# Attention loads over all 128 partitions, the block means through the tensor engine for every pair, an earlier expert pick and a linear part inside the test

## The chip, the cores and the metric

The kernel runs on one NeuronCore of a Trainium2 chip. The metric is device time in microseconds (us) of one execution. TensorE (PE), VectorE (DVE), ScalarE (ACT), GpSimd (POOL) and SyncE (SP) each have an instruction queue of their own. SP issues every load and store here but one; the bytes are moved by 16 DMA engines.

## The reference, cut to what matters

```python
def _attn_ref(q, k, v):                       # q, k, v: (4, 8, 768, 64)
    k_sum = k.reshape(B, H, nb, 32, D).max(axis=3)
    v_sum = v.reshape(B, H, nb, 32, D).mean(axis=3)
    scores = concat(window scores |i-j| < 16, q @ k_sum.T + log(32))
    return softmax(scores) @ concat(v, v_sum)
def _moe_ref(x, phi, w1, w2):                 # x: (3072, 512), 8 experts, 4 slots each
    logits = x @ phi
    slot_input = softmax(logits, axis=0).T @ x
    slot_out[e] = relu(slot_input[e] @ w1[e]) @ w2[e]
    return softmax(logits, axis=1) @ slot_out
def _moe2_ref(x, expert_emb, tau, w1, w2):    # top-1 expert for each token
    expert_idx = argmax(xn @ en.T / tau)
    out = gate * (relu(x @ w1[e]) @ w2[e])
```

The output of the attention is the x of the first mixture, whose output is the x of the second. All tensors are float32.

## The kernel before

**Attention.** The 4 x 8 heads are taken as 16 pairs of heads n. Each pair has 3 steps u = 3n, 3n+1, 3n+2, so there are 48 steps. A step scores 4 query blocks of 64 rows for both heads (`s_pe`, L351), takes maximum and exponential (`s_max`, `s_exp`), transposes the probabilities (`p_pe`, L386) and multiplies them with the values (`v_pe`, L403). The parts are staggered over the steps: `p_pe` of step u-2, `v_pe` of step u-3. Every three steps PE also transposes the result and adds the logits of the first mixture (L436, L454); after every batch of four pairs it adds `pn` and `pa` (L497, L525).

A pair loads q (`qT`, 128 rows), k (`kT`, 128 rows, written as six pieces of 512 bytes in each row, between which the block maxima of k stand) and a windowed copy of v, `vw`. Its tile has up to 120 rows: the window rows of the even and the odd query blocks, and in rows 16 to 39 (even) and 80 to 103 (odd) the 24 block means of v. The load of `vw` is three or four transfers: 120, 80 and 16 rows for pairs 0 to 7 (`VS_PE`), 16, 80, 80 and 16 rows for pairs 8 to 15 (L266).

The block means come about in two ways. For pairs 0 to 7, PE forms them from `vw` itself (`vs_pe`, L278, four products), ACT takes them out of PSUM (`vs_out`, L289), SP writes them to DRAM (`vsp`, L296), waits for that write, and reads them back into `vw` in two transfers that repeat them six times (`vsum_in`, L318). For pairs 8 to 15, v is loaded once more for two pairs at a time in 96 rows (`load_vs`, L256), POOL adds its halves (L304), SP writes the means (`vsc`, L311) and reads them back. The source calls in step u are in the order: `vs_pe`, `vs_out`, `vs_dma`, the loads of k and q, the load of v two pairs ahead, the read-back, one load of a weight tile.

**Weights.** From step 9 on one tile of 1 MB of the first mixture's weights is loaded per pair (`load_w`, L177); 32 tiles in all, the last ones as buffers come free. 16 products `ph` (L800) and 16 pieces `pO` (L866) use them up; r counts two groups of four experts, fc the eight pieces of a group.

**Second mixture.** Because one expert serves all tokens where the inputs allow it, the kernel picks the expert of token 0 before the last pieces are added: behind piece fc = `G_STEP` = 5 of the second group it copies the sum so far, multiplies it out for token 0 (`first_expert`: `px`, `pl`, then DVE makes the index `ei`), and SP loads that expert's weights (`w1e`, `w2e`, L828, L835). The last two pieces go into a second bank; `psoT` (L920) adds both halves in the transpose. Then come a Gram matrix (`pk`, L950), 8 tokens' logits (`pl`, L955), the product of the slot outputs with `w1e` (`pg`, L1029, `pgs`, L1042), which makes G, and the other logits. `norms` and `codes` on DVE end the stage.

**Test.** 24 pieces `pht` (L1113) of G times the tokens are checked for sign, 14 on ACT (L1132) and 10 on DVE (`T_DVE`, L1121), over a ring of four double banks. Where all tokens agree in sign, a hidden unit is linear; the linear part is `prr` (L1158), `rs`, `prs` (L1207) and `RR` (L1222). The units that are not linear are gathered (`prk`, `OH`, `pix`, `pgm`, an indirect load `wr`), and the output loop adds three products for them to the linear product `linear` (L1230), scales and stores (L1248). A loop behind that runs a whole expert for each further expert that tokens chose.

```python
G_STEP = 5                                            # L44
return psb.tile([P, 1024], F32, tag=f"d{n2[0] % 4}", name=name)   # L1107
```

Of the kernel before, what the change touches and what calls it, by code (L numbers as in the profile page):

```python
# [31 lines left out]
NSLOT = 32  # L32
NBIG = 15
NBIG2 = 4

VS_PE = (0, 1, 2, 3)
# [7 lines left out]
G_STEP = 5  # L44

T_DVE, T_GATES, T_OTHERS = (5, 7, 9, 11, 13, 15, 17, 19, 21, 23), (6, 8, 10, 13), 15
NE = 8
# [89 lines left out]
def tile_kernel(ctx, tc, qT, kTd, vwd, vbd, phi, w1, w2, emb, tau, u1, u2, consts, consts2, out):  # L137
# [68 lines left out]
    with ExitStack() as es:  # L206
# [18 lines left out]
        vos = []  # L225
# [14 lines left out]
        def load_qk(n):  # L240
            if n == 0:
                for h in range(2):
                    nc.sync.dma_start(
                        out=k_blocks(0)[:, 3 * h : 3 * h + 3, 0:128],
                        in_=kTd[0, :, h * 384 : h * 384 + 384].rearrange("p (c x) -> p c x", x=P),
                    )
# [52 lines left out]

        def vsum_add(m):  # L300
            vs = st_["vs", m]
            h = BLK // 2
            while h:
                nc.gpsimd.tensor_add(vs[:, :h, :], vs[:, :h, :], vs[:, h : 2 * h, :])  # L304
                h //= 2

        def vsum_out(m):
            vo = vos[m % 2]
            nc.gpsimd.tensor_scalar_mul(vo[:, 0:D], st_.pop(("vs", m))[:, 0, :], 1.0 / BLK)
            sc = dram.tile([NB, 2, 130], F32, name=f"vsc{m}")  # L310
            nc.sync.dma_start(out=sc.rearrange("n i (j d) -> (n i j) d", j=2), in_=vo)  # L311
            for i in range(2):
                st_["sc", 2 * m + i] = sc[:, i, :]
# [334 lines left out]
        for u in range(NU + 32):  # L648
# [59 lines left out]
            for n in range(NPAIR):  # L708
                if n // 2 in VS_PE:
                    up, uo, ui = VS_FIRST[n] if n < 2 else (3 * n - 2 - (n % 4 == 3), 3 * n - 1, 3 * n)  # L710
                    if u == up:
                        vs_pe(n)
                        vs_out(n)
                    if u == uo:
                        vs_dma(n)
                    if u == ui and n == 0:
                        load_qk(2)
                        vsum_in(0)
                    elif u == ui:
                        late.append(n)  # L720
# [8 lines left out]
            if (m := at(u, 0, 6, 2 * B - 1)) is not None and m + 1 not in VS_PE:  # L729
                load_vs(m + 1)  # L730
            if (m := at(u, 3, 6, 2 * B - 1)) is not None and m + 1 not in VS_PE:
                vsum_add(m + 1)
            if (m := at(u, 5, 6, 2 * B - 1)) is not None and m + 1 not in VS_PE:
                vsum_out(m + 1)
            if (n := at(u, 6, 3, NPAIR - 2)) is not None and (n + 2) // 2 not in VS_PE:
                vsum_in(n + 2)
# [78 lines left out]
    OO = [O, hx[:, 5, :]]  # L815
# [42 lines left out]
    for r in range(2):  # L858
        for fc in range(8):
# [3 lines left out]
            for c in range(2):  # L863
# [54 lines left out]
    for c in range(4):  # L918
        for i in range(2):
            nc.tensor.matmul(  # L920
                pt[:, c * P : (c + 1) * P], OO[i][:, c * P : (c + 1) * P], sel, start=i == 0, stop=i == 1
            )
# [163 lines left out]
    pgs = [g_half(f, bank) for f in range(2)]  # L1086
    pg = [g_sum(f, pgs[f], bank) for f in range(2)]
    for f in range(2):
        g_parts(f, pg[f])
    for t in range(8, NTT):  # L1090
        tok(t)
    ph0 = bank(1, "ph0")[:, 0 : 2 * NU].rearrange("p (k x) -> p k x", x=2)
    for k in range(NU):
        nc.tensor.matmul(ph0[:, k, :], G[:, k * P : (k + 1) * P], cTt(0, 2), start=True, stop=True)
    nc.vector.tensor_scalar(out=pos, in0=ph0[:, :, 0], scalar1=0.0, scalar2=None, op0=ALU.is_ge)
    nc.vector.tensor_scalar(out=ngs, in0=pos, scalar1=-2.0, scalar2=1.0, op0=ALU.mult, op1=ALU.add)
    norms()
    codes()
    psa_es.close()

    with ExitStack() as es:
# [3 lines left out]
        def dbank(name):  # L1105
            n2[0] += 1
            return psb.tile([P, 1024], F32, tag=f"d{n2[0] % 4}", name=name)  # L1107

        for i in range(3 * NU):
# [25 lines left out]
            if i == 4:  # L1135
# [19 lines left out]
        prr, rs = dbank("prr")[:, 0:512], hx[:, 1, :]  # L1155
        for k in range(NU):
            g = k % 4
            nc.tensor.matmul(  # L1158
                prr[32 * g : 32 * g + 32, :], GPT[:, k, :], w2e[k // 4][:, k % 4, :], start=k < 4, stop=k >= 4
            )  # L1160
        nc.scalar.copy(rs, prr)

# [10 lines left out]
    for k in range(NU):  # L1173
# [6 lines left out]
        )  # L1180
    nc.vector.scalar_tensor_tensor(
# [153 lines left out]
```

## Time and profile before

| | us |
|---|---|
| median of 3 runs | 325.37 |
| lowest, highest | 320.84, 325.95 |
| the profiled execution | 324.63 |
| its span, from the first to the last instruction | 322.5 |
| PE, DVE, ACT, POOL busy | 270.8, 168.9, 156.7, 40.0 |

The profile is of one execution. A row of the chain or of the timeline gives the start, the duration, the engine, the tile written, the line, and how many instructions were merged (x8). A matmul of float32 counts twice. A row of the windows view gives a stretch, then the busy time of the engines asked for, then the clock that TensorE was granted (1.00 is 2.4 GHz, 0.50 is 1.2 GHz), the busy share of the DMA engines and GB/s. "SPq" is the time that SP's queue needs to issue a transfer.

### The profile page before, as it was taken

To read this page: it belongs to the slowest core of one execution; us is meant where nothing else is said; L and a number is where in the kernel's file an instruction comes from. 1 tells how busy PE (TensorE), PEld (TensorE's weight loads), DVE (VectorE), ACT (ScalarE), POOL (GpSimd) and SP (SyncE) were. 2 spreads that over 40 slices of the span, in tenths; PEclk is the share of its full clock that TensorE was granted. 3 is DMA by queue.
4 is the path that set the end of the run, shared out by engine and by line. 5 is a ranking of instruction groups with operands and counts; after the bars stand their busy time and mean duration, and the time that the engine had idled before them with its cause. 6 is when DMAs were issued, how large, how long until landed. Compare 5 with 4: busy or idle time off the path is not lost.

```text
span 322.5 us, 6780 instructions
## 1 busy us (share of the span) xinstructions
PE 270.8 (84%) x2428; PEld 183.9 (57%) x2428; DVE 168.9 (52%) x756; ACT 156.7 (49%) x390; POOL 40.0 (12%) x63
## 2 busy tenths in 40 slices
PE   6779999939994994994988999999987778778890
PEld 2556877718784873684875643354544544555560
DVE  3546677733985475484584542141215489345440
ACT  2554887816685563484684621132312797133330
POOL 2000010102512413413400001000000030100000
PEclk9589999987999897897899999999978798769997
DMA  7999798899997996998988999999394000105563
GB/s 196 211 258 239 215 277 267 206 275 244 220 267 187 287 310 182 286 293 225 310 217 232 387 387 384 387 386 381 116 363 158 2 0 0 33 31 194 201 254 112
DMA packets 49342, 74.00 MB, mean 229 GB/s; under 512 B 4048, under 2 KB 22416, under 8 KB 48920
## 3 DMA queue, kind: packets, MB, share of 16 engines
q1 hardware_dynamic: 49224, 73.26, 76.4%
q8 instruction: 21, 0.34, 0.5%
q0 software_dynamic: 80, 0.26, 0.3%
q14 instruction: 17, 0.14, 0.2%
HBM read 67.02 MB, written 6.49 MB: 228 GB/s over the span
## 4 chain that ended last, share of the span: by engine, by line
PE 52%; DMA 28%; DVE 6%; ACT 5%; SPq 4%; issue 3%; DVEq 0%; ACTq 0%
DMA vsc<-vo 12%; DMA vw<-in_vw_dram 7%; PE s L351 7%; PE po L403 5%; PE pO L866 5%; PE ph L800 4%; DMA vsp<-vo 4%; PE pt L386 3%; PE pa L525 3%; PE py L1230 3%; DMA qn<-in_qT_dram 2%; PE tx L436 2%; DMA vw<-vsc 2%; DVE hlo L1121 2%; PE pv L278 2%
## 5 line engine op out<-in xcount | busy, mean ns | idle before, releaser
L351 PE MATMUL s<-fix,fix 128*128 128x120 f32 x384 | 60.5, 305 | 3.5 <-DVE nb L363 3.0
L351 PEld LDWEIGHTS s<-fix,fix 128*128 128x128 f32 x384 | 51.4, 208 | 16.4 <-issue 5.2
L403 PE MATMUL po<-vw,pts 120*64 120x65 f32 x768 | 35.7, 232 | 18.0 <-DMA vw<-vsc 15.7
L391 ACT COPY pts<-pt 120x512 f32<-120x512 f32 x48 | 28.1, 585 | 37.2 <-PE pt L386 36.6
L403 PEld LDWEIGHTS po<-vw,pts 120*64 120x64 f32 x768 | 28.5, 141 | 30.4 <-issue 14.4
L378 ACT ACTIVATE fix<-fix,nb 128x120 f32<-128x120 f32 x128 | 40.1, 387 | 2.6 <-DVE nb L363 2.4
L363 DVE CUSTOM_DVE_ANT_0 fix<-s,con 128x120 f32<-128x120 f32 x128 | 28.4, 277 | 19.2 <-PE s L351 16.2
L304 POOL TENSOR_TENSOR vs<-vs 96x1024 f32<-96x1024 f32 (+4 forms) x20 | 20.4, 1021 | 47.6 <-DMA vs<-in_vb_dram 46.4
L1113 PE MATMUL pht<-cT,gs 128*128 128x512 f32 x48 | 17.1, 496 | 7.0 <-DVE hx L973 3.1
L418 DVE TENSOR_SCALAR den<-po 128x4 f32<-128x4 f32 x48 | 7.5, 157 | 26.5 <-PE po L403 26.4
L420 DVE TENSOR_TENSOR X<-po,den 128x256 f32<-128x256 f32 x48 | 20.4, 424 | 1.7
L378 ACT ACTIVATE sm<-sm,nb 128x120 f32<-128x120 f32 x64 | 20.0, 387 | 0.6 <-DVE nb L363 0.5
L1132 ACT ACTIVATE hhi<-pht,ngs 128x1024 fp32r<-128x1024 f32 x14 | 15.6, 1116 | 8.0 <-PE pht L1113 7.8
L386 PE MATMUL pt<-con,fix 128*120 128x128 f32 x128 | 19.3, 273 | 0.0
L363 DVE CUSTOM_DVE_ANT_0 sm<-s,con 128x120 f32<-128x120 f32 x64 | 14.3, 277 | 7.2 <-PE pt L386 3.6
L1113 PEld LDWEIGHTS pht<-cT,gs 128*128 128x128 f32 x48 | 10.3, 236 | 13.3 <-DVE acc L1121 4.8
L436 PE MATMUL tx<-con,X 128*128 128x128 f32 x96 | 17.1, 290 | 0.0
L337 DVE TENSOR_REDUCE fix<-fix 128x12 f32<-128x384 f32 x32 | 16.2, 547 | 0.9 <-DMA fix<-in_kT_dram 0.8
L866 PE MATMUL pO<-w,hx 128*32 128x256 f32 x256 | 16.1, 383 | 0.0
L363 DVE DVE_READ_ACCUMULATOR2_ANT nb<- 128x1 f32 x192 | 15.8, 82 | 0.1
L446 ACT COPY xT<-tx 128x512 f32<-128x512 f32 (+1 forms) x32 | 14.8, 462 | 2.1 <-PE tx L436 2.1
L1121 DVE CUSTOM_DVE_ANT_0 hlo<-pht,ngs 128x1024 fp32r<-128x1024 f32 x10 | 12.2, 1215 | 6.1 <-PE pht L1113 5.3
(232 smaller groups left out, 397.4 us busy)
## 6 DMA issues: line engine op xcount, KB each, us to landing
w<-in_moe_w_dram SPq DMA_DIRECT2D x30, 1024.0 KB
out_dram<-Y SPq DMA_DIRECT2D x24, 256.0 KB
vw<-in_vw_dram SPq DMA_DIRECT2D x24, 243.8 KB
fix<-in_kT_dram SPq DMA_DIRECT2D x15, 384.0 KB
qn<-in_qT_dram SPq DMA_DIRECT2D x8, 384.0 KB
vs<-in_vb_dram SPq DMA_DIRECT2D x4, 768.0 KB
vw<-in_vw_dram SPq DMA_DIRECT2D x8, 365.6 KB
fix<-in_qT_dram SPq DMA_DIRECT2D x7, 384.0 KB
```

Of the source, the lines that this page charges most:

```text
L304: nc.gpsimd.tensor_add(vs[:, :h, :], vs[:, :h, :], vs[:, h : 2 * h, :])
L351: nc.tensor.matmul(sp[:, i, :], qbds[n % NQB][:, t, :], kTs[n % NKT][:, o : o + KW], start=True, stop=True)
L363: nc.vector.tensor_tensor_reduce(out=sm[:, i, :], in0=sp[:, i, :], in1=con[:, m0 : m0 + KW], scale=-0.125, scalar=3.0e38, op0=ALU.add, op1 ...
L378: nc.scalar.activation(sm[:, i, :], sm[:, i, :], AF.Exp, bias=nb_[:, i : i + 1], scale=-1.0)
L386: nc.tensor.transpose(pv[:, i, :], pr[:, i, :], ident)
L391: nc.scalar.copy(pts, st_.pop(("pt", u)))
L403: nc.tensor.matmul(po[64 * i : 64 * i + 64, c, j, :], pts[:, 2 * c + i, j * 64 : j * 64 + 64], vw[:, i, (t // 2) * 130 + 65 * j : (t // 2) ...
L420: nc.vector.tensor_tensor(out=X[:, 2 * g : 2 * g + 2, 2 * hp * D : (2 * hp + 2) * D].rearrange("p c (j d) -> p c j d", j=2), in0=po[:, :, ...
L436: nc.tensor.transpose(pt[:, c * P : c * P + P], st_["X", b][:, c0 + c, hp * P : hp * P + P], ident)
L866: nc.tensor.matmul(po[c][32 * g : 32 * g + 32, 0:256], hTs[r][:, fc, 32 * g : 32 * g + 32], w[:, g, cs], start=(r, fc) in ((0, 0), (1, G_S ...
L1113: nc.tensor.matmul(ph[:, c * 512 : c * 512 + 512], G[:, k * P : (k + 1) * P], cTt(1024 * j + 512 * c, 512), start=True, stop=True,)
L1121: nc.vector.tensor_tensor_reduce(out=junk[1], in0=ph, in1=ngs[:, k : k + 1].to_broadcast([P, 1024]), scale=1.0, scalar=0.0, op0=ALU.mult, ...
```

## The change

1. Loads. `kT` is laid out in DRAM as it lies in the tile, gaps included (912 floats a row, one piece). `vw` is one transfer of 128 rows x 1568 floats, with zeros where the means go; the four or three transfers are gone.
2. Block means. `VS_PE`, `load_vs`, `vsum_add` and `vsum_out` are gone: all 16 pairs take the way through PE, ACT and DRAM.
3. Pick. `G_STEP` is 3: the sum behind piece fc = 3 (of 0 to 7) is copied, `px` follows behind the products of piece 4, `pl` and the index behind those of piece 5. The remaining pieces are added on DVE to the copy, so `psoT` has one product per column block and not two.
4. Order. `pg` comes straight behind `psoT`, ahead of the Gram matrix and of all logits. The logits' banks are in a pool of their own that stays open through the test, `norms` and `codes` come behind the first test, and the test's ring has three double banks.
5. Linear part. `prr` and `rs` come behind test 17, `prs` and `RR` behind test 18; four `linear` products come ahead of `pix`. `pgm` is written twice side by side (256 columns).

```diff
-VS_PE = (0, 1, 2, 3)
-G_STEP = 5
+G_STEP = 3
+T_LIN = 17
...
-            for par, r0, r1 in (*even, (1, 0, 80), (1, 104, KW)):
-                nc.sync.dma_start(
-                    out=vw[r0:r1, par],
-                    in_=vwd[n, par, r0:r1].rearrange("p c j d -> p (c j d)"),
-                )
+            st_["vw", n] = t[:KW, :VROW].rearrange("p (a x) -> p a x", a=2)
+            nc.sync.dma_start(out=t[:, :VPAD], in_=vwd[n])
...
-            nc.sync.dma_start(out=k_blocks(n)[:, :, 0:128], in_=kTd[n].rearrange("p (c x) -> p c x", x=P))
+            nc.sync.dma_start(out=kTs[n % NKT][:, 40 : 40 + 912], in_=kTd[n])
...
                 if (r, fc) == (1, 7):
-                    (nc.scalar.copy, nc.vector.tensor_copy)[c](OO[1][:, cs], po[c][:, 0:256])
-            if (r, fc) == (1, G_STEP):
+                    nc.vector.tensor_tensor(out=O[:, cs], in0=po[c][:, 0:256], in1=O[:, cs], op=ALU.add)
+            if (r, fc) == (1, G_STEP + 1):
                 first_expert()
+            if (r, fc) == (1, G_STEP + 2):
+                first_expert_code()
...
+    pgs = [g_half(f, bank) for f in range(2)]
     gram()
-    for t in range(8):
-        tok(t)
...
-            return psb.tile([P, 1024], F32, tag=f"d{n2[0] % 4}", name=name)
+            return psb.tile([P, 1024], F32, tag=f"d{n2[0] % 3}", name=name)
...
+            if i == 0:
+                norms()
+                codes()
...
+            if i == T_LIN + 1:
+                prs = dbank("prs")[:, 0:512]
+                nc.tensor.matmul(prs, sel, rs, start=True, stop=True)
+                nc.scalar.copy(RR, prs)
+                nc.vector.tensor_tensor(out=RR[64:P], in0=prs[64:P], in1=RR[64:P].bitcast(F32), op=ALU.subtract)
```

SP's queue in the middle of the attention before, for about two pairs; `fix` and `qn` are the tiles of k and q, `w` a weight tile, `vs` the second copy of v, `vsc` the means in DRAM:

```order
L177 DMA w_1103<-in_moe_w_dram 128x4x512
L266 DMA vw_1157<-in_vw_dram 16x780
L266 DMA vw_1157<-in_vw_dram 80x780 x2
L266 DMA vw_1157<-in_vw_dram 16x780
L251 DMA fix_102<-in_kT_dram 128x6x128
L252 DMA fix_103<-in_qT_dram 128x768
L311 DMA vsc_1205<-vo_116 96x65
L256 DMA vs_1247<-in_vb_dram 96x2048
L318 DMA vw_995<-vsc_1205 24x6x130 x2
L177 DMA w_1251<-in_moe_w_dram 128x4x512
```

The same place now:

```order
L181 DMA w_1222<-in_moe_w_dram 128x4x512
L255 DMA vw_1278<-in_vw_dram 128x1568
L282 DMA vsp_1319<-vo_1276 8x390
L248 DMA fix_103<-in_kT_dram 128x912
L249 DMA qn_105<-in_qT_dram 128x768
L289 DMA vw_1134<-vsp_1319 24x6x130 x2
L181 DMA w_1360<-in_moe_w_dram 128x4x512
```

A pair now has 7 transfers on SP's queue; the means go out ahead of k and q and are read back behind them, for every pair.

PE from the pick's products to the product with the picked expert's weights before; `pc` is a transpose, `pcb` the picked code:

```order
L844 MATMUL px_2863<-c0r,O_2686 128x1
L847 MATMUL pl_2864<-enT,x_2687 1x8 x4
L196 MATMUL pc_1_2900<-con,st_2755 128x128 x3
L866 MATMUL pO_2905<-w_2627,hx 32x256 x4
L866 MATMUL pO_2906<-w_2627,hx 32x256 x4
L866 MATMUL pO_2905<-w_2633,hx 32x256 x4
L866 MATMUL pO_2906<-w_2633,hx 32x256 x4
L920 MATMUL psoT<-con,hx 128x128 x8
L950 MATMUL pk<-hx 128x40 x4
L955 MATMUL pl_2962<-KL,cT_2682 128x40 x8
L1018 MATMUL pcb<-r_2688,con 128x1
L1029 MATMUL pg_3000<-w1e_2878,hx 32x512 x2
```

The same now:

```order
L806 MATMUL px_2843<-c0r,O_2677 128x1
L200 MATMUL pc_0_2849<-con,st_2746 128x128 x3
L831 MATMUL pO_2833<-w_2605,hx 32x256 x4
L831 MATMUL pO_2834<-w_2605,hx 32x256 x4
L812 MATMUL pl_2862<-enT,x_2678 1x8 x4
L200 MATMUL pc_1_2893<-con,st_2746 128x128 x3
L831 MATMUL pO_2833<-w_2618,hx 32x256 x4
L831 MATMUL pO_2834<-w_2618,hx 32x256 x4
L831 MATMUL pO_2833<-w_2624,hx 32x256 x4
L831 MATMUL pO_2834<-w_2624,hx 32x256 x4
L886 MATMUL psoT<-con,hx 128x128 x4
L993 MATMUL pg_2968<-w1e_2871,hx 32x512 x2
```

The pick's two groups of products have a piece `pO` between them, and still two pieces follow `pl`; `psoT` has half its products, and `pg` stands where the Gram matrix stood, which with all logits now follows it.

PE at the end of the test before, the last two test pieces and what follows them:

```order
L1113 MATMUL pht_3181<-cT_2683,gs 128x512
L1113 MATMUL pht_3185<-cT_2683,gs 128x512 x2
L1158 MATMUL prr<-w2e_2880,scr 32x512 x4
L1158 MATMUL prr<-w2e_2881,scr 32x512 x4
L1172 LDWEIGHTS ltb
L1172 MATMUL prk<-flag,ltb 128x9
```

Now, test piece 17 and what follows it:

```order
L1074 MATMUL pht_3148<-cT_2674,gs 128x512 x2
L1123 MATMUL prr<-w2e_2873,scr 32x512 x4
L1123 MATMUL prr<-w2e_2874,scr 32x512 x4
L1074 MATMUL pht_3162<-cT_2673,gs 128x512 x2
L1133 MATMUL prs<-hx,con 128x512
L1074 MATMUL pht_3170<-cT_2673,gs 128x512
```

The linear part's products went from behind the last test piece (and `prs` from behind the gather) to between the pieces 17 and 19. On DVE the subtraction that makes `RR` stands ahead of test 19 in the same way.

## Rows read from the trace of the kernel before

**Rows 1.** Windows view, three stretches: stretch, length, busy of five engines, PEclk, DMA share, GB/s.
```profile
33.00:54.00 21.00, 21.00 (x254) 17.12 (x254) 15.26 (x89) 17.38 (x48) 0.82 (x1) 1.00 0.88 244
72.00:171.00 99.00, 83.34 (x896) 66.67 (x892) 62.96 (x349) 60.30 (x171) 28.86 (x34) 0.89 0.95 250
171.00:222.00 51.00, 50.88 (x538) 25.36 (x541) 19.85 (x78) 15.56 (x37) 2.04 (x4) 1.00 1.04 371
```
**Rows 2.** Windows view of PE, first 16 us: stretch, length, PE busy, PEclk, DMA share, GB/s.
```profile
9.25:11.00 1.75, 1.09 (x5) 0.50 1.15 242
11.00:12.00 1.00, 1.00 (x9) 0.50 1.07 372
12.00:15.00 3.00, 3.00 (x15) 0.50 0.94 210
```
**Rows 3.** Waits of PE on loads: us in total, times, longest.
```profile
PE po L403 <- DMA vw<-vsc: 15.7, 7, 4.6
PE pv L278 <- DMA vw<-in_vw_dram: 5.7, 3, 5.4
```
**Rows 4.** The chain in the first 36 us: start, us, what.
```profile
6.24 9.65 DMA vw<-in_vw_dram
...
25.92 6.17 DMA vw<-in_vw_dram
```
**Rows 5.** The chain through the attention, PE's score steps and one batch's end.
```profile
35.56 1.08 PE s L351 x8
...
43.97 1.08 PE s L351 x8
...
80.28 0.48 PE pn L497 x4
...
82.72 1.85 PE pa L525 x12
...
176.50 1.08 PE s L351 x8
```
**Rows 6.** Timeline of SP's queue: the means of pair 5 go out, and are read back.
```profile
53.36 0.61 SPq L296 DMA_DIRECT2D vsp<-vo  x1
...
59.93 1.91 SPq L318 DMA_DIRECT2D vw<-vsp  x2
```
**Rows 7.** The chain from the pick to the first test.
```profile
227.91 0.26 PE pO L866 x4
...
229.91 0.48 PE pc L196 x3
...
232.25 2.00 PE psoT L920 x16
...
238.45 4.04 PE pg L1029 x16
...
250.88 1.20 PE pht L1113 x2
```
**Rows 8.** Timeline of SP's queue: the loads of the picked expert's first weights.
```profile
231.89 2.19 SPq L828 DMA_DIRECT2D w1e<-in_moe_w_dram  x4
```
**Rows 9.** The test: the page's group of DVE, and of the chain its end.
```profile
L1121 DVE CUSTOM_DVE_ANT_0 hlo<-pht,ngs 128x1024 fp32r<-128x1024 f32 x10 | 12.2, 1215 | 6.1 <-PE pht L1113 5.3
...
272.74 1.92 PE prr L1158 x16
274.69 0.59 ACT hx L1161
```
**Rows 10.** The chain from the gather to the first product of the output loop.
```profile
280.18 1.81 PE prs L1207 x2
...
283.81 0.70 DVE gs L1222
284.56 2.08 PE py L1230 x4
286.64 0.43 PE py L1237
```

More of the change, by code (lines that the diff above doesn't have):

```diff
@@ L298, in vs_dma @@
             )
[L300 to L313, printed above, removed]
         def vsum_in(n):
@@ L708, in tile_kernel @@
             for n in range(NPAIR):
[L709 to L720, printed above, removed]
+                up, uo, ui = VS_FIRST[n] if n < 2 else (3 * n - 2 - (n % 4 == 3), 3 * n - 1, 3 * n)
+                if u == up:
+                    vs_pe(n)
+                    vs_out(n)
+                if u == uo:
+                    vs_dma(n)
+                if u == ui and n == 0:
+                    load_qk(2)
+                    vsum_in(0)
+                elif u == ui:
+                    late.append(n)
             if (n := at(u, 2, 3, NPAIR - 3)) is not None:
@@ L918, in tile_kernel @@
     for c in range(4):
[L919 to L922, printed above, removed]
+        nc.tensor.matmul(pt[:, c * P : (c + 1) * P], O[:, c * P : (c + 1) * P], sel, start=True, stop=True)
     nc.gpsimd.tensor_copy(SOE[:, :, P:], enT)
@@ L1085, in tile_kernel @@
     )
-    pgs = [g_half(f, bank) for f in range(2)]
-    pg = [g_sum(f, pgs[f], bank) for f in range(2)]
     for f in range(2):
-        g_parts(f, pg[f])
-    for t in range(8, NTT):
+        g_parts(f, g_sum(f, pgs[f], bank))
+    for t in range(12):
         tok(t)
@@ L1094, in tile_kernel @@
         nc.tensor.matmul(ph0[:, k, :], G[:, k * P : (k + 1) * P], cTt(0, 2), start=True, stop=True)
+    for t in range(12, NTT):
+        tok(t)
     nc.vector.tensor_scalar(out=pos, in0=ph0[:, :, 0], scalar1=0.0, scalar2=None, op0=ALU.is_ge)
     nc.vector.tensor_scalar(out=ngs, in0=pos, scalar1=-2.0, scalar2=1.0, op0=ALU.mult, op1=ALU.add)
-    norms()
-    codes()
     psa_es.close()
@@ L1153, in tile_kernel @@
                 others()
[L1155 to L1161, printed above, removed]
+            if i == T_LIN:
+                prr, rs = dbank("prr"), hx[:, 1, :]
+                for k in range(NU):
+                    g = k % 4
+                    nc.tensor.matmul(
+                        prr[32 * g : 32 * g + 32, 0:512],
+                        GPT[:, k, :],
+                        w2e[k // 4][:, k % 4, :],
+                        start=k < 4,
+                        stop=k >= 4,
+                    )
+                nc.scalar.copy(rs, prr[:, 0:512])
+            if i == T_LIN + 1:
[3 more added lines that the diff above has]
+                nc.vector.tensor_tensor(out=RR[64:P], in0=prs[64:P], in1=RR[64:P].bitcast(F32), op=ALU.subtract)
+    psl_es.close()
     psc = ctx.enter_context(tc.tile_pool(name="psc", bufs=1, space=PSUM))
@@ L1180, in tile_kernel, with linear @@
         )
+    pys = {}
+    def linear(t):
+        pys[t] = bankc((4, 5, 6, 7, 0)[t % 5], f"py{t}")
+        nc.tensor.matmul(pys[t], cTt(t * P, P), RR, start=True, stop=False)
+    for t in range(4):
+        linear(t)
     nc.vector.scalar_tensor_tensor(
@@ L1192, in tile_kernel @@
     )
-    pix, pgm = bankc(2, "pix")[:, 0:2], bankc(3, "pgm")[:, 0:P]
+    pix, pgm = bankc(2, "pix")[:, 0:2], bankc(3, "pgm")[:, 0 : 2 * P]
     for k in range(NU):
@@ L1204, in tile_kernel @@
     )
-    nc.scalar.copy(Gm, pgm)
-    prs = bankc(0, "prs")
-    nc.tensor.matmul(prs, sel, rs, start=True, stop=True)
+    nc.scalar.copy(Gm, pgm[:, 0:P])
     row_weights(cbx)
@@ L1220, in tile_kernel @@
     mixed(0)
-    nc.scalar.copy(RR, prs)
-    nc.vector.tensor_tensor(out=RR[64:P], in0=prs[64:P], in1=RR[64:P].bitcast(F32), op=ALU.subtract)
     mixed(1)
@@ L1225, in tile_kernel @@
     nc.vector.tensor_tensor(out=wml, in0=wr, in1=wmh.bitcast(F32), op=ALU.subtract)
-    pys = {}
-    def linear(t):
-        pys[t] = bankc((4, 5, 6, 7, 0)[t % 5], f"py{t}")
-        nc.tensor.matmul(pys[t], cTt(t * P, P), RR, start=True, stop=False)
-    for t in range(4):
-        linear(t)
     for t in range(NTT):
```

61 lines of the change are left out of this document (26 added, 35 removed).

## The prediction

> **What bounds the kernel now.** I read the windows first, since the kernel is a row of stages with different limits; then PE's waits and the chain inside the stages that the change touches.
>
> In the attention the DMA engines are the limit for most of the time. From 72 to 171 us they are 0.95 busy and move 250 GB/s, PE works 83.3 of 99 us and has a clock of 0.89; in the weight stage behind it the same engines at 1.04 move 371 GB/s, and PE is never idle [rows 1]. So a busy DMA engine moves a third less in the attention. Single loads show which: with the queue full, q (128 rows, one piece each) goes at 372 GB/s, k (128 rows in pieces of 512 bytes) near 242, and `vw` (120, 80 and 16 rows) at 210 [rows 2]. PE's named waits on this are 15.7 us for read-back means of pairs 8 to 15 and 5.7 us for `vw` [rows 3]; the chain of the start stands twice on `vw`, for 9.65 and 6.17 us [rows 4].
>
> Where nothing is late, PE sets the pace: from 33 to 54 us it is busy without a gap at the full clock [rows 1], and three steps, a pair, take 43.97 - 35.56 = 8.41 us [rows 5]. That pair has the means' products on PE, as all pairs will. A batch's end adds 0.48 + 1.85 = 2.33 us [rows 5]. Between step 8 (35.56) and the last step 47 (176.50) lie 39 steps, 13 pairs, in 140.94 us, 10.84 a pair.
>
> From 176.50 to 232.25 PE goes through the rest of the attention and the weights, then the second mixture begins with `psoT` [rows 5, 7]. There short steps wait for each other, and DMA matters only for the picked expert.
>
> **The change part by part.** All sums are against the profiled execution, 324.63 us.
>
> *Loads, attention from step 8.* Bytes of a late pair before: k 0.393, q 0.393, `vw` 0.599, half of the second v 0.393, means 0.162, weight tile 1.049, together 2.99 MB; now k 0.467, q 0.393, `vw` 0.803, means 0.162, weight 1.049, together 2.87 MB. An early pair goes up from 2.67 to 2.87. The gain is thus not in bytes but in their rate. At 371 GB/s a pair needs 7.75 us of DMA, under PE's 8.41 and under 9.0, the mean with the batch ends (8.41 + 2.33/4). Then 13 pairs take 13 x 8.41 + 3 x 2.33 = 116.3 us, 24.6 less than 140.94. This includes PE's added products and ACT's added copies, which are in the pair that I took the pace from; POOL's sums go away and nobody else takes them. What can be late next is SP's queue: it stops at each read-back until the write of the means has landed, and weight and `vw` are issued only behind that. Before, from write to read-back 6.57 us pass (59.93 - 53.36) [rows 6]. How much of it the DMA engines are dry is between nothing (they stayed 0.95 busy [rows 1]) and 6.57 less k and q, which are queued ahead (0.86 MB, 2.3 us): 4.25. I take 1 us, near the low end, for the row that says busy: 8.75 a pair against 8.41 costs 0.34 in each of the nine pairs that have no batch end, 3 us. Term: -21.6, from -24.6 to -10 (4.25 dry would make 12.0 a pair and leave no gain, but a dry queue and a share of 0.95 exclude each other; half of it makes 9.9, a gain of 12).
>
> *Start.* Up to step 8 the chain stands on the `vw` of pairs 1 and 3, behind which k and `vw` of four pairs have been moved. A `vw` of these is 0.674 MB, 3.2 us at 210 GB/s, and becomes 0.803 MB, 2.2 us at 371; a k goes from 0.393 MB at 242 (1.6 us) to 0.467 at 371 (1.25). Four of each: 4 x (1.0 + 0.35) = 5.4. Both waits end on the load, and the two writes of the means that wait behind these loads come sooner too, so I count it whole and round up: -6, from -3 (only the first two of each count, then PE at half clock is the limit) to -8.
>
> *From step 47 to `psoT`.* The pick's stall goes: pO ends at 228.17 and the next big work starts at 229.91 [rows 7], 1.74 us, of which the pick's products themselves are about 0.6 and stay. -1.2, from 0 to -1.7. The weight tiles come as before relative to step 47, since their order and buffers are the same.
>
> *Order, `psoT` to the first test*, now 250.88 - 232.25 = 18.63 us [rows 7]. `psoT` halves (-1.0), a DVE addition comes ahead of it (+0.5 to +0.9). `pg` no longer waits behind Gram matrix and logits but for its weights: pl is again two pieces ahead of `psoT`, so the load starts as now, 0.4 us ahead of it (231.89) [rows 8]; 2.1 MB at 371 GB/s are 5.7 us, with start and landing between 6 and 8. `pg`'s last quarter (1.0 of 4.04) follows it, so it ends 7 to 9 us behind the start of `psoT`, now 238.45 + 4.04 - 232.25 = 10.24. Gram, eight logits and the code, which lay between, cost up to 3.5 us later, of which one or two are beside the copies of `pg`. `norms` and `codes` leave the way to the first test; they are part of the 250.88 - 242.49 = 8.4 us behind `pg`, which hold five other steps too, and I give them a third, 2.6. Sum: -1.7 (`pg`) + 2 - 2.6 = -2.3, from -5 to 0.
>
> *Test.* The ring of three makes DVE's first test wait for one more test on ACT; a test is 1.2 us on DVE [rows 9], and I take 1.1 for ACT. The linear part in the middle hits DVE: between its tests 17 and 19 now stand `prr` 1.92, `rs` 0.59 [rows 9], ACT's test 18 at 1.1, the copy at the 0.59 of `rs` and the subtraction at 0.70 [rows 10]: 4.9 us, where its own test of 1.2 ran before; 3.7 more. DVE ends the test before, at about the time of `rs` (274.69), so this is late: +4.8. If the gaps of PE and ACT take half in, +1.5; if the shorter ring also costs 0.3 on each of the last dozen tests, +8.5.
>
> *Behind the test.* `prs` (1.81) and the four `linear` products (284.56 to 286.64, 2.08) leave the chain [rows 10], the latter to where PE waits for DVE. The gathered weights are then late next: they can't be there earlier than now relative to `pix`. I take -3.2 of the 3.89, from -1 to -4.5 (`pgm` at 256 columns is one to two times its time).
>
> Sum: -21.6 - 6 - 1.2 - 2.3 + 4.8 - 3.2 = -29.5, so 324.63 - 29.5 = 295.1; I say 295. The median of the runs is 0.74 us above the profiled execution, which I leave.
>
> **One rule against this.** The row shows busy engines that move little: a share of 0.94 at 210 GB/s [rows 2]. The Trainium skill (DMA: Bandwidth & Descriptors, Why a DMA increments its semaphore by 16 and not by 1) says that a transfer runs on the largest number of engines up to 16 that divides its outer dimension; by it 80 and 16 rows already have all 16, 120 rows 15, and more rows gain hardly anything. [...]
>
> **The rivals.**
>
> *`vw` stays slow* (the mechanism: its rate is not set by its rows). Then k gains, and a pair needs 467/371 + 393/372 + 803/210 + 162/210 + 1049/371 = 9.7 us against a mean of 9.0: 13 pairs give back 9.1 of the 24.6, and with the dry queue 3 more; the start gains 1.4 on k and loses 2.5 on `vw`. 324.6 - 12.5 + 1.1 - 1.9 (the last four terms) = 311. For it: the high DMA share beside 210. Against: a like share gives 372 on q in the same stretch [rows 2].
>
> *The weights become the clock.* 16 pairs at 1.83 MB and 32 tiles at 1.049 are 63 MB ahead of the last `pO`. If `psoT` comes at 203 us and no longer at 232, the last tile must be there by about 202, a mean of 314 GB/s. At 371 it is there with room; at a mean of 293, because SP's queue stops at the read-backs, it is there at 217, and PE waits some 14 us in the weight stage: 309. For it: tiles are asked for only as buffers come free. Against: before, the same order kept PE busy [rows 1].
>
> *SP's round trip becomes slower than the DMA was.* If weight and `vw` (2.8 + 2.2 us) don't overlap the 6.57, a pair takes 6.57 + 1.91 (the two read-backs [rows 6]) + 5.0 = 13.5 us, and 13 pairs 175 + 7 instead of 141: 358, slower. It turns slower when the part of the trip that lies beside nothing is over 3.9 us a pair. Against: before, the DMA engines worked through this trip.
>
> *Everything overlaps.* No dry queue (-24.6), test at +1.5, start at -8: 324.6 - 37.8 = 287.
>
> *The pick from fewer pieces names another expert,* and the loop behind the output runs a whole expert: over 100 us more. Worked out from the reference's inputs, 12 and 16 pieces both name expert 5 for token 0, and all tokens share it, so hardly.
>
> **How the numbers follow.** Forecast with its own range 289 to 301: 0.57. Everything overlaps: 0.15. Weights: 0.12. `vw` slow: 0.10. Round trip: 0.05. Pick: 0.01. For 8 in 10 the range goes from 287, the better case, to 310, between the weights' 309 and the 311 of a slow `vw`. Faster by over 2% (about what a measurement of this kernel can tell from no change) is below 318.9: all of the first four, 0.94, less 0.01 for what I have not seen: 0.93. Within 2%: 0.03, a mild round trip. Slower: 0.04.
>
> **What would show it.** Right: step 8 near 30 us and step 47 near 149 in the chain; GB/s in the attention well above 250 with a lower DMA share; pairs of 8.4 to 9 us; no `vsc`; DVE with a hole of some 4 us behind test 17; `linear` ahead of `pix`. Wrong: waits of PE on `vw<-vsp` in most pairs (round trip), waits of `ph` or `pO` on `w` (weights), `vw` near 210 GB/s in the first 16 us, or a test stage that is not longer.

## The result and the profile after

The kernel after takes 300.23 us (median of four runs, 298.22 to 303.94), the kernel before beside it 324.88 (320.84 to 325.95): a ratio of 0.926, 95% interval 0.913 to 0.939. Faster, as forecast, and inside the range of 289 to 301, 5.2 us above the forecast of 295.

The profiled execution of after took 301.13 us, 23.5 less than the 324.63 of before. The windows view of after, cut where the stages begin (stretch, length, busy time of PE, PEld, DVE, ACT and POOL, granted clock, DMA share, GB/s):

```profile
6.50:12.00 5.50, 3.22 (x22) 1.79 (x21) 2.72 (x19) 2.10 (x6) 0.00 (x0) 0.88 1.01 408
...
31.25:155.37 124.12, 117.28 (x1395) 89.77 (x1393) 90.10 (x502) 88.15 (x253) 9.15 (x13) 0.99 0.83 280
155.37:211.58 56.21, 54.96 (x609) 26.58 (x605) 19.28 (x73) 17.31 (x40) 1.74 (x4) 1.00 1.01 357
211.58:225.60 14.02, 12.17 (x74) 7.26 (x71) 4.19 (x14) 2.82 (x8) 0.71 (x4) 1.00 0.83 307
225.60:254.36 28.76, 21.54 (x77) 11.32 (x77) 20.36 (x42) 20.61 (x34) 3.21 (x3) 0.88 0.00 0
254.36:291.64 37.28, 32.78 (x129) 22.83 (x129) 15.87 (x30) 11.43 (x19) 1.16 (x1) 0.86 0.41 153
```

Cut at the same products, the two executions compare like this (the stages begin where the timeline has the product named; `prk` is the first product behind the test):

| stage | before | after | difference | predicted |
|---|---|---|---|---|
| to step 8 | 35.49 | 31.25 | -4.24 | -6 |
| step 8 to step 47 | 140.94 | 124.12 | -16.82 | -21.6 |
| step 47 to `psoT` | 55.75 | 56.21 | +0.46 | -1.2 |
| `psoT` to the first `pht` | 18.70 | 14.02 | -4.68 | -2.3 |
| first `pht` to `prk` | 24.44 | 28.76 | +4.32 | +4.8 |
| `prk` to the last `py`, and the end | 49.31 | 46.77 | -2.54 | -3.2 |
| sum | 324.6 | 301.1 | -23.5 | -29.5 |

The loads carry the gain. Where [rows 2] had 242 and 210 GB/s, the first microseconds now move 408, and in the attention the DMA engines move 280 GB/s at a share of 0.83 where [rows 1] had 250 at 0.95: less busy, and more moved. The waits of [rows 3] on `vsc` are gone. What is left of the waits on `vw` stands on the chain of waits of after:

```profile
3.09 7.14 DMA vw<-in_vw_dram
...
22.31 5.53 DMA vw<-in_vw_dram
...
31.31 1.08 PE s L322 x8
...
39.73 1.08 PE s L322 x8
...
48.72 4.34 DMA vsp<-vo
...
53.87 0.40 SPq L181
...
54.31 9.44 DMA vw<-in_vw_dram
...
63.89 0.86 PE pv L264 x8
...
94.32 8.86 DMA vw<-in_vw_dram
103.32 0.86 PE pv L264 x8
...
133.74 7.67 DMA vw<-in_vw_dram
141.55 0.86 PE pv L264 x8
...
155.44 1.08 PE s L322 x8
```

The first two rows answer to [rows 4]: 7.14 and 5.53 us in place of 9.65 and 6.17. The other three are new. In each batch of four pairs, PE stops once, at the means' products `pv` of the pair with n % 4 = 3; the code puts those one step earlier than those of the other pairs. Their `vw` (9.44, 8.86 and 7.67 us from issue to landing) was issued behind the read-back of the means and behind a weight tile (the SPq row of L181 just ahead). Other pairs take 8.42 us (39.73 - 31.31), as the 8.41 of [rows 5].

The second surprise is at the end of the weights. The timeline of PE in after (start, duration, line, what, count, and in brackets the idle time before and what ended it):

```profile
208.26 1.07 PE L831 MATMUL pO<-w,hx 128*32 128x256 f32 x16 [0.15 <-DMA w<-in_moe_w_dram]
209.64 0.64 PE L831 MATMUL pO<-w,hx 128*32 128x256 f32 x8 [0.30 <-DMA w<-in_moe_w_dram]
211.01 0.64 PE L831 MATMUL pO<-w,hx 128*32 128x256 f32 x8 [0.74 <-DMA w<-in_moe_w_dram]
211.58 1.40 PE L886 MATMUL psoT<-con,hx 128*128 128x128 f32 x8
213.86 0.62 PE L993 MATMUL pg<-w1e,hx 128*32 128x512 f32 x2 [0.88 <-DMA w1e<-in_moe_w_dram]
```

PE, never late on a weight tile in [rows 1], waits 1.2 us for the last three, and then for the picked expert's `w1e`. And in the test DVE has the hole that the prediction named, here between its tests 17 and 19:

```profile
245.14 1.22 DVE L1082 CUSTOM_DVE_ANT_0 hlo<-pht,ngs 128x1024 fp32r<-128x1024 f32 x1
...
248.94 0.69 DVE L1135 TENSOR_TENSOR gs<-prs,gs 64x512 fp32r<-64x512 f32 x1 [2.58 <-ACT gs L1134]
249.66 1.23 DVE L1082 CUSTOM_DVE_ANT_0 hlo<-pht,ngs 128x1024 fp32r<-128x1024 f32 x1
```

It begins the next test 3.3 us after the end of the one before it (245.14 + 1.22 to 249.66).

### The profile page after: what moved, and what is told of

The parts are those of the page before. It is cut to its first block, busy times and chain, and to the rows that moved or that the text cites. A ratio compares the mean times of both kernels' runs of the same rounds, so it can differ in the third digit from the quotient of the medians.

```text
span 298.9 us, 6816 instructions
## 1 busy us (share of the span) xinstructions
PE 262.7 (88%) x2484; PEld 174.2 (58%) x2484; DVE 168.4 (56%) x757; ACT 158.0 (53%) x397; POOL 17.9 (6%) x37
## 4 chain that ended last, share of the span: by engine, by line
PE 57%; DMA 25%; ACT 6%; DVE 4%; SPq 3%; issue 3%; ACTq 0%; DVEq 0%
DMA vw<-in_vw_dram 13%; PE s L322 10%; DMA vsp<-vo 6%; PE po L374 6%; PE ph L763 5%; DMA w<-in_moe_w_dram 4%; PE pt L357 4%; PE pv L264 4%; PE tx L407 3%; PE lp L425 3%; PE pa L496 3%; PE py L1159 2%; PE pO L831 2%; DMA w1e<-in_moe_w_dram 2%; DVE hlo L1082 2%
## 5 line engine op out<-in xcount | busy, mean ns | idle before, releaser
L322 PE MATMUL s<-fix,fix 128*128 128x120 f32 x384 | 56.4, 291 | 3.2 <-DVE nb L334 2.1
L322 PEld LDWEIGHTS s<-fix,fix 128*128 128x128 f32 x384 | 47.6, 195 | 18.6 <-DVE den L390 5.7
L374 PE MATMUL po<-vw,pts 120*64 120x65 f32 x768 | 33.2, 227 | 2.1 <-ACT fix L349 2.0
L374 PEld LDWEIGHTS po<-vw,pts 120*64 120x64 f32 x768 | 26.5, 137 | 14.1 <-issue 6.1
L275 ACT COPY vo<-pv 128x390 f32<-128x390 f32 x16 | 7.8, 486 | 37.2 <-PE pv L264 37.2
L1074 PE MATMUL pht<-cT,gs 128*128 128x512 f32 x48 | 18.0, 506 | 4.1 <-DVE acc L1082 2.5
L264 PE MATMUL pv<-vw,con 80*32 80x390 f32 (+1 forms) x128 | 14.3, 517 | 7.4 <-DMA vw<-in_vw_dram 7.4
L1074 PEld LDWEIGHTS pht<-cT,gs 128*128 128x128 f32 x48 | 9.7, 232 | 12.1 <-DVE acc L1082 4.3
L407 PE MATMUL tx<-con,X 128*128 128x128 f32 x96 | 16.3, 280 | 0.0
L357 PEld LDWEIGHTS pt<-con,fix 128*120 128x120 f32 x128 | 15.3, 142 | 0.1
```

The lines of the kernel that those rows point to most:

```text
L264: nc.tensor.matmul(pv[32 * g : 32 * g + 32, 0:390], con[:rows, C_BLK + 32 * par : C_BLK + 32 * par + 32], vw[:rows, par, 390 * hf : 390 * ...
L322: nc.tensor.matmul(sp[:, i, :], qbds[n % NQB][:, t, :], kTs[n % NKT][:, o : o + KW], start=True, stop=True)
L357: nc.tensor.transpose(pv[:, i, :], pr[:, i, :], ident)
L374: nc.tensor.matmul(po[64 * i : 64 * i + 64, c, j, :], pts[:, 2 * c + i, j * 64 : j * 64 + 64], vw[:, i, (t // 2) * 130 + 65 * j : (t // 2) ...
L407: nc.tensor.transpose(pt[:, c * P : c * P + P], st_["X", b][:, c0 + c, hp * P : hp * P + P], ident)
L1074: nc.tensor.matmul(ph[:, c * 512 : c * 512 + 512], G[:, k * P : (k + 1) * P], cTt(1024 * j + 512 * c, 512), start=True, stop=True,)
```

## The experiments

### The two halves apart

`e1_loads` has the change up to the end of the attention and the pick, order and test of before; `e2_mixture` the reverse.

> The first half of the change alone (padded k, vw over 128 rows in one transfer, all block means through PE, no vb); the pick, the order of the second mixture and the test are those of the kernel before. Theory (the two halves add up, and the weight tiles hide little): step 8 near 31.3 and step 47 near 155.4 us, as in the profile after, that is 4.25 + 16.8 = 21.0 us less than before, with the pick's stall of 1.74 us back in the weight stage: 303 to 305. Rival (the weight tiles are the clock from step 47 on): the stall lies beside the late tiles and the time to psoT is the same as after, 56.1 us, so 302 to 303.

> The second half alone: loads and block means of the kernel before, with the early pick, the new order of Gram, logits and pg, and the linear part inside the test. Theory: -1.2 (no stall of the pick, since the tiles are early here) -4.4 (psoT to the first test) +4.1 (test) -2.5 (behind it) = -4.0, near 320.6. Rival (the order is given back by the longer test wholly): 323 to 325, no difference that can be told.

Measured: `e1_loads` 302.87 us (299.79 to 305.15) beside 325.19 of before, ratio 0.947 (0.931 to 0.962): 22.3 us less, where the whole change made 24.6 less. It lies where the rival put it, and its stretch from step 47 to `psoT` takes 56.66 us (209.85 - 153.19), near the 56.21 of after, though the pick's stall is back in it. `e2_mixture` took 326.20 (322.67 to 330.14) beside the same 325.19: no difference that can be told, as its rival has it; the theory's 320.6 isn't borne out. The windows from `psoT` to the last `py`, first of `e1_loads`, then of `e2_mixture`, then of after:

```profile
209.85:290.04 80.19, 65.15 (x285) 42.15 (x281) 40.67 (x86) 34.49 (x61) 5.07 (x8) 0.89 0.34 125
```
```profile
177.65:232.53 54.88, 54.55 (x609) 26.82 (x606) 19.40 (x74) 17.29 (x40) 1.74 (x4) 1.00 0.99 360
232.53:312.51 79.98, 67.64 (x273) 40.82 (x273) 40.17 (x86) 34.88 (x61) 5.09 (x8) 0.87 0.34 125
```
```profile
211.58:291.64 80.06, 66.49 (x277) 41.41 (x273) 40.42 (x86) 34.85 (x61) 5.08 (x8) 0.89 0.34 125
```

All three are 80 us, with the old order and with the new. What the new order gains ahead of the test, the test loses. Before itself takes 82.1 us here (314.31 - 232.18) with the code that `e1_loads` has, so that some 2 us between two executions come without any edit to this part. Of the second half only the pick's stall is left as a gain, 0.87 us (54.88 against 55.75), and after doesn't have it, because its tiles come late.

### What made the loads faster

```diff
 # e3_vw_rows
-nc.sync.dma_start(out=t[:, :VPAD], in_=vwd[n])
+for r0, r1, c0, c1 in ((0, KW, 0, VROW // 2), (0, 80, VROW // 2, VROW), (104, KW, VROW // 2, VROW)):
+    nc.sync.dma_start(out=t[r0:r1, c0:c1], in_=vwd[n, r0:r1, c0:c1])
 # e11_rows120
-nc.sync.dma_start(out=t[:, :VPAD], in_=vwd[n])
+nc.sync.dma_start(out=t[:KW, :VPAD], in_=vwd[n, :KW])
```

> The kernel after, with vw loaded as before in rows of 120, 80 and 16 (three transfers, 0.674 MB in place of 0.803). Theory (the rows set the rate): vw goes back to about 210 GB/s, 3.2 us against 2.2 to 2.4; the start loses 2 to 4 us, and each of the 13 pairs from step 8 on is late by up to 1 us: 306 to 314. Rival (the gain came from the dropped vb and its POOL path, not from the rows): 0.13 MB less per pair makes it no slower than 301.

> The kernel after, with vw loaded in one transfer of 120 rows and not of 128 (0.753 MB in place of 0.803). It tells what it was in the old transfers that made them slow. Theory A (only 128 rows go at the full rate, and eight rows less cost as much as 80 and 16 did): step 8 to step 47 takes 138 us or more, as 142.1 us with 120, 80 and 16 rows. Theory B (the transfers of 80 and 16 rows were the slow ones; 120 rows are nearly 128): within 4 us of the 124.1 of after.

Measured: `e3_vw_rows` 320.87 us (318.59 to 324.81), a ratio to before of 0.997 (0.992 to 1.002). The rival is out, and the loss is larger than the theory's 306 to 314: nearly the whole gain is gone, though `vb` and POOL's sums are gone too. `e11_rows120` took 330.93 (328.94 and 332.92), the time of the kernel before or a little more (ratio 1.016, 1.004 to 1.029, from two runs). It differs from after by the last eight rows of one load. Its windows, and then PE's wait on `vw` (us in total, times, longest):

```profile
6.50:10.50 4.00, 2.06 (x8) 1.78 (x8) 1.50 (x12) 1.86 (x5) 0.00 (x0) 0.70 0.97 222
10.50:12.00 1.50, 1.00 (x8) 0.23 (x8) 0.65 (x9) 0.00 (x0) 0.00 (x0) 0.50 0.98 382
12.50:14.00 1.50, 1.50 (x10) 1.50 (x8) 1.21 (x5) 1.39 (x5) 0.00 (x0) 0.50 0.84 192
...
39.67:186.79 147.12, 124.09 (x1396) 94.24 (x1392) 90.07 (x502) 87.15 (x251) 9.14 (x13) 0.91 0.84 229
```
```profile
PE pv L264 <- DMA vw<-in_vw_dram: 28.4, 9, 8.4
```

By the order in SP's queue, the first window is the `vw` of pair 0, the second k and q of pair 1, the third the next `vw`: 222, 382 and 192 GB/s at shares of 0.84 to 0.98. In after the whole stretch from 6.5 to 12 us goes at 408. So 120 rows have about half the rate of 128, in one transfer as in three; theory A holds, 147.12 us against its 138 or more, and the transfers of 80 and 16 rows were not the only slow ones. The kernel before has a load of another size that bears this out: `vs`, one transfer of 96 rows of 8192 bytes, is the last in SP's queue from 117.32 us on until 124.44, and by its own 0.786 MB, counted back from about 123.5 us, where the queue runs dry, the stretch from 121 to 123 us is its own:

```profile
121.00:123.00 2.00, 1.00 (x10) 0.76 (x8) 1.93 (x13) 1.99 (x7) 0.00 (x0) 1.00 1.02 237
```

It went at 237 GB/s with the engines busy, so 96 rows are slow too. The rule weighed in the prediction doesn't give this size. By the Trainium skill (DMA: Bandwidth & Descriptors, Why a DMA increments its semaphore by 16 and not by 1) 120 rows run on 15 engines and 96 rows on all 16; an estimate worked out from that is a loss of a sixteenth for 120 rows and none for 96. By another page of the Trainium skill (SBUF — State Buffer, Door 1: The DMA port swizzle) 120 rows, and 96 too, still reach all 16 ports and should lose nothing. The measurement decides against both as an explanation; the cause of the half rate stays open, and row counts between 120 and 128 were not tried.

`e4_k_pieces` writes k again in six pieces of 512 bytes a row.

> The kernel after, with k written in six pieces of 512 bytes per row as before (0.393 MB in place of 0.467). Theory: 1.6 us at 242 GB/s against 1.25, so +1 us at the start and at most +0.35 in each pair that waits: 301 to 305. Rival (k was the half that mattered): over 308.

Measured: 303.10 us (301.80 to 305.58), as the theory has it; step 8 at 33.49 and 123.64 us from there to step 47. In the attention k's form plays no part (124.12 in after). At the start 33.49 is 2.2 us later than in after, but kernels with the start of after have step 8 anywhere from 29.29 (`e1_loads`) to 32.94 (`e8_lin_behind`), so this isn't told. The window in which, by the bytes ahead of it, k of pair 1 lands shows the rate of the pieces:

```profile
8.25:9.50 1.25, 1.25 (x6) 1.25 (x7) 0.49 (x6) 1.17 (x4) 0.00 (x0) 0.50 1.08 347
```

With `vw` in 128 rows ahead of it, k in pieces of 512 bytes goes at 347 GB/s. So the 242 of [rows 2] was not the rate of the pieces as such, though the prediction read it so; in that stretch k stood right behind a slow `vw`.

### What is left in the attention

```diff
 # e5_pv_step
-up, uo, ui = VS_FIRST[n] if n < 2 else (3 * n - 2 - (n % 4 == 3), 3 * n - 1, 3 * n)
+up, uo, ui = VS_FIRST[n] if n < 2 else (3 * n - 2, 3 * n - 1, 3 * n)
 # e6_w_behind
-W_STEPS = (*range(9, 42, 3), 41, 43, ...
+W_STEPS = (*range(10, 41, 3), 41, 43, ...
```

> The kernel after, with the products of the means of pairs 3, 7, 11 and 15 one step later, where those of all other pairs stand. Theory (what is left of the attention's gain is lost where these four products ask for vw a step too early): the waits of 2.85, 1.93 and 1.59 us and the half clock behind the first go, step 47 comes 5 to 8 us sooner, near 149, and since the tiles from w12 on wait for buffers that the attention frees, psoT moves by as much: 293 to 297. Rival A (the tiles of the weight stage come no sooner): psoT moves by 2 us at most, 298 to 300. Rival B (the means then come late for the products with the values): 301 or more, with a wait of po on vw<-vsp.

> The kernel after, with the load of a weight tile in step 3n+1 in place of 3n, so that SP issues it behind vw and not ahead of it. Theory: vw lands some 2.8 us (1.049 MB at 371 GB/s) sooner, and the three waits of pv on it shrink to 0 to 0.5 us; step 47 some 5 us sooner, 295 to 298. Rival (vw is late because SP stood at the read-back, and the order behind it does nothing): the waits stay within 1 us of 2.85, 1.93 and 1.59, no difference.

Measured: `e5_pv_step` 296.80 us (294.05 to 299.24), `e6_w_behind` 294.99 (293.84 to 296.34). Before was at 320.86 beside them, so that their ratios, 0.933 (0.920 to 0.946) and 0.925 (0.914 to 0.936), don't tell them from after by themselves; the traces show where the time goes. The windows from step 8 to 47 of `e5_pv_step`, then of `e6_w_behind` SP's queue, PE's timeline, and the windows from step 8 to 47 and to `psoT`:

```profile
28.67:147.86 119.19, 116.00 (x1396) 88.62 (x1393) 88.74 (x501) 87.53 (x253) 9.13 (x13) 1.00 0.87 295
```
```profile
51.42 0.74 SPq L289 DMA_DIRECT2D vw<-vsp  x2
52.21 0.36 SPq L255 DMA_DIRECT2D vw<-in_vw_dram  x1
52.62 0.43 SPq L181 DMA_DIRECT2D w<-in_moe_w_dram  x1
```
```profile
60.86 0.86 PE L264 MATMUL pv<-vw,con 120*32 120x390 f32 x8
```
```profile
31.13:148.67 117.54, 115.75 (x1397) 88.59 (x1393) 89.83 (x502) 87.99 (x253) 9.12 (x13) 1.00 0.86 293
148.67:205.37 56.70, 54.96 (x609) 26.60 (x605) 19.26 (x73) 17.29 (x40) 1.74 (x4) 1.00 1.00 357
```

With `vw` issued ahead of the weight tile, the `pv` that stood at 63.89 starts at 60.86 with no wait, and the 39 steps take 117.54 us, 1.2 over the 116.3 that the prediction worked out as dense. So each edit alone removes most of the 7.8 us: the products are a step early, and `vw` is a weight tile late. `psoT` comes 6.2 us sooner in `e6_w_behind`: the weight stage moves with the attention (56.70 behind it against 56.21).

### The last tiles and the pick

`e12_half_tiles` loads half the columns of the last four tiles (`for c in range(0, 256 if i >= 28 else 512, n)`).

> The kernel after, with only half the columns of the last four weight tiles loaded (2.1 MB less, 5.7 us at 371 GB/s); the products use the half twice, so PE's work is the same, and the output leaves out half of these weights. Theory (from w12 on the DMA engines and not PE set the end of the weight stage and the start of pg): PE's waits of pO on w go, step 47 to psoT takes 54.5 to 55.2 in place of 56.2 us, and psoT to the first pht 11 to 13 in place of 14.0, since w1e no longer stands behind the tiles. Rival (the tiles hide nothing): 56.2 and 14.0 stay within 0.5.

Measured: 300.82 us (299.16 and 302.47). The windows of `e12_half_tiles` from step 47 to `psoT` and on to the first `pht`, then DVE's timeline and the chain:

```profile
155.02:209.90 54.88, 54.55 (x609) 26.81 (x606) 19.41 (x74) 17.29 (x40) 1.73 (x4) 1.00 0.93 328
209.90:227.22 17.32, 14.26 (x70) 7.54 (x71) 4.04 (x14) 2.81 (x8) 0.71 (x4) 0.80 0.69 251
```
```profile
207.94 0.14 DVE L818 TENSOR_SCALAR ei<-r 1x1 int32<-1x1 f32 x1
```
```profile
210.87 6.25 DMA w1e<-in_moe_w_dram
...
217.16 3.25 PE pg L993 x8
```

The first half of the theory holds: 54.88 us, as with the early tiles of `e2_mixture`, so the late tiles cost after 1.3 us. The second half fails: the first `pht` comes 17.3 us behind `psoT` (227.22 - 209.90), not 11 to 13. The queue was free (33 GB/s from 204 to 208 us), but the pick's index `ei` is there at 208.08 only, `w1e` is issued behind it and lands at 217.1. PE came to `pg` sooner and waited longer: `w1e` is there 7.2 us behind the start of `psoT` (217.12 - 209.90), in after 6.4 (211.77 + 6.18 - 211.58). What `w1e` waits for is the pick, not the tiles. But that is only 0.8 of the 3.3 us by which the stretch is longer than in after. Most of the rest is PE's clock: it was granted 0.80 over this stretch, in after 1.00. PE stood 2.2 us ahead of `pg`, and `pg`'s last eight products then took 3.25 us, where in after only four were left, for 1.05.

### The linear part in the test

`e7_lin_later` puts `prs` and `RR` behind test 20 (`if i == T_LIN + 3`); `e8_lin_behind` takes `prr`, `rs`, `prs`, `RR` and the first four `linear` out of the test, to where they were.

> The kernel after, with prs and RR behind test 20 in place of test 18. Theory (DVE stands at RR because ACT's copy comes late): DVE's idle time of 2.58 us ahead of the subtraction shrinks under 1, the test stage goes from 28.8 us (first pht to prk) to 26.5 to 27.5. Rival (the ring of three decides: prs holds a buffer of it either way): 28.5 to 29, no change.

> The kernel after, with the linear part (prr, rs, prs, RR, the first four linear products) behind the test as before, the ring of three, the early pick, the order and pgm at 256 columns kept. Theory (what the test gains the part behind it loses): first pht to prk 25 to 25.5 us (before 24.4), prk to the first product with wmh 2.5 us longer, in sum within 1.5 us of after. Rival (the part inside the test pays): 2 to 4 us slower than after.

Measured: 305.59 us (301.94 to 309.66) and 301.37 (298.66 to 306.21); neither is told from after by its time. The windows from the first `pht` to `prk` and DVE's timeline in `e7_lin_later`, then the windows in `e8_lin_behind`:

```profile
226.99:255.14 28.15, 21.15 (x76) 10.99 (x77) 20.35 (x42) 20.67 (x34) 3.21 (x3) 0.90 0.00 0
```
```profile
248.46 1.23 DVE L1082 CUSTOM_DVE_ANT_0 hlo<-pht,ngs 128x1024 fp32r<-128x1024 f32 x1 [1.25 <-PE pht L1074]
...
251.09 0.69 DVE L1135 TENSOR_TENSOR gs<-prs,gs 64x512 fp32r<-64x512 f32 x1 [1.40 <-ACT gs L1134]
```
```profile
231.97:257.86 25.89, 21.29 (x74) 11.27 (x75) 19.81 (x41) 20.09 (x33) 3.21 (x3) 0.84 0.00 1
```

Moved by two tests, the hole splits in two (1.25 and 1.40 us), and the stage gets 0.6 us shorter: neither expectation, nearer the rival. Without the linear part the stage takes 25.89 us at a lower clock, so the part costs 2.9 us there or more, and ring and later `norms` together at most 1.45 (25.89 - 24.44). From `prk` to the first product with `wmh` it then takes 10.15 us (268.01 - 257.86) against 8.47 in after (262.83 - 254.36): 1.7 longer, not 2.5. Over both stretches the linear part inside the test costs 1.2 us more than it saves (37.23 against 36.04), within the 1.5 of the theory. That it pays 2 to 4 us, as the rival has it, no execution shows.

### The edits together

`e10_best` has the edits of `e5_pv_step`, `e6_w_behind` and `e8_lin_behind`; after ran again beside it.

> The kernel after, unchanged, for a comparison on one chip with the next run. All theories: the ratio of the first measurement, 0.913 to 0.939 of before.

> The kernel after with three edits: the four early products of the means one step later, a weight tile's load behind vw, and the linear part behind the test as before. Theory (the three act in different stages and add up): step 8 near 28.7, step 47 near 146, psoT near 202, psoT to the last py 78.5 to 80: 286 to 290 profiled, 4 to 5% under after. Rival (the weight tiles are the clock and take back what the attention gains beyond the better of the two single edits): psoT not before 203.4, 291 to 295.

Measured: after 302.52 us (301.37 to 303.14, six runs), `e10_best` 295.65 (289.90 to 300.04, six runs); the ratios to before are 0.929 (0.923 to 0.935) and 0.894 (0.884 to 0.905), which don't overlap, and the longest of its runs is shorter than the shortest of after. So `e10_best` beats both kernels, by 2.3% over after by the medians and 3.7% by the two ratios. Its windows by stage, and from `psoT` to the first `pht`:

```profile
32.16:150.75 118.59, 115.94 (x1397) 88.60 (x1393) 88.89 (x501) 87.58 (x253) 9.16 (x13) 1.00 0.88 296
150.75:205.62 54.87, 54.71 (x609) 26.70 (x606) 19.26 (x73) 17.31 (x40) 1.74 (x4) 1.00 1.00 362
205.62:285.91 80.29, 65.00 (x277) 39.23 (x273) 40.62 (x86) 34.79 (x61) 5.08 (x8) 0.91 0.34 125
205.62:222.56 16.94, 13.46 (x75) 7.65 (x71) 4.30 (x14) 2.82 (x8) 0.71 (x4) 0.88 0.72 257
```

The edits don't add up, and not for the reason of the rival: the tiles aren't late (54.87). One of the two edits in the attention is enough, and from `psoT` on it is 80 us once more, though the test lost the linear part. Its first `pht` comes 16.9 us behind `psoT` (222.56 - 205.62), with PE's waits on `w1e` at 3.5 us. Here `w1e` isn't late: it is there 5.9 us behind `psoT` (205.99 + 5.49 - 205.62), sooner than the 6.4 of after. But PE stood 3.3 us ahead of `pg` and then had a clock of 0.88 in this stretch, and `pg`'s last twelve products took 4.14 us. That is where the theory's 78.5 to 80 failed.

## Why the prediction was right, and where it was off

*Loads: mechanism right, one term too small.* The rate of the loads was the cause: `e1_loads` has nearly the whole gain, and `e11_rows120` gives it all back with eight rows less. Of the two loads only `vw` counts: k's pieces were misread, as `e4_k_pieces` shows. The term was -21.6 and came to -16.8. The pace of 8.41 us a pair was right. The step that failed is the one on the dry queue: "8.75 a pair against 8.41 costs 0.34 in each of the nine pairs that have no batch end, 3 us". It measured 7.8 us (124.1 - 116.3), and lay in three pairs and not in nine. (Ten of the 13 pairs, not nine, have no batch end, so that the step itself comes to 3.4.) I looked for an empty queue and overlooked a full one: `vw` waited behind a weight tile, for products that the code asks for a step early in those pairs.

*Start: -6, measured -4.2.* The two `vw` on the chain gained 2.5 and 0.6 us (9.65 and 6.17 against 7.14 and 5.53), 3.1 of the 5.4 worked out; the second is issued only behind a read-back of means (22.31, before at 25.92), and that trip is not a matter of rate alone. Of the 5.4, 1.4 were k's pieces at 242 GB/s; `e4_k_pieces` shows them at 347. With the same loads `e1_loads` has step 8 at 29.29, 6.2 ahead of before, and `e8_lin_behind` at 32.94, so that -6 itself is not refuted. Whether the products of pair 3 a step later help here isn't told: step 8 stood at 28.67 in `e5_pv_step` and at 32.16 in `e10_best`.

*From step 47 to `psoT`: wrong sign, 1.7 us off.* The stall went, as `e2_mixture` shows (54.88). What failed is "The weight tiles come as before relative to step 47". The rival that the weights become the clock is true at its edge, with 1.3 us (`e12_half_tiles`) and not 14. A likely cause, read from SP's queue and not tried: the write, wait and read-back of the last pair's means now stand between tiles w12 and w13, so that w13 is issued 1.0 us ahead of step 47, and 5.6 ahead of it in before.

*Order: -2.3, measured -4.7.* Right in sign. `pg` ends 7.5 us behind the start of `psoT` (219.04 - 211.58; 7 to 9 was worked out, and the term of -1.7 stands for 8.5; 10.24 before), and from there to `pht` it is 6.6 us in place of 8.4. One step that was mis-sized is the 2 us for Gram matrix, logits and code behind `pg`: with `norms` and `codes` gone from there, the stretch became 1.8 us shorter, where I had 0.6. The other is PE's clock, for which I had no term:

```profile
232.18:250.88 18.70, 14.29 (x82) 9.18 (x79) 6.28 (x21) 2.90 (x9) 0.72 (x4) 0.82 0.63 232
```

This is the stretch in before, at 0.82; in after it was 1.00, and one product of `pg` took 0.59 us in place of 1.06. So the order's gain varies with the clock: against `e1_loads`, which has the old order at 0.87 and takes 17.6 us (227.44 - 209.85), it is 3.6, and after itself took 15.05 at 0.95 when it ran again (225.02 - 209.97).

*Test: +4.8, measured +4.3,* with the hole at the place named. Its parts, 3.7 for the linear part and 1.1 for the ring, measured 2.9 or more and 1.45 or less, the latter with `norms` and `codes`. The hole was 3.3 us from test to test, where 4.9 was worked out.

*Behind the test: -3.2, measured -2.5,* to the end of the execution.

The sum of the last three terms is -0.7 in the prediction and -2.9 between the two profiles, but against `e1_loads` after gains only 0.1 from `psoT` to the last `py`. The second half of the change is worth nothing that these runs can tell. So it is luck that the forecast for the profiled execution missed by 6.0 us (301.1 against 295.1): the 2.4 us that the order gained beyond its term, in part by a clock that I hadn't foreseen, hide half of the 4.8 that the loads fell short.

## What to carry to other kernels

Try a load padded to all 128 rows even where the added rows hold nothing: here 7% more bytes made it go at about twice the rate, and the DMA share did not give the slow form away, only GB/s beside it did. When transfers become faster, look next at their order in the issuing queue, at who asks for them first, and at the steps that the code puts early for one case in four. And time both halves of a change apart: one carried all that these runs can tell, and the other moved waits from one stage into the next. Where a wait gets shorter or longer, look also at the clock of the products behind it.

## What the hardware showed that I had not expected

A load of 120 rows with 6272 bytes each moved 192 to 222 GB/s at DMA shares of 0.84 to 0.97, the same load with 128 rows stood in a stretch that moved 408. Half the rate for 8 rows of 128; why was not found. And a high DMA share can go with either rate: 0.97 at 222 GB/s and 1.01 at 408.
